# Sliding-window attention and a gated feed-forward layer on one core: q and k of six batches turned by DMA in 128-row chunks

## The chip, the cores and the metric

The kernel runs on one core of a Trainium2 chip. Its time is the device time of one launch, in microseconds (us). The engines have queues of their own and run in order: TensorE (PE in the profile; its weight loads are PEld), VectorE (DVE), ScalarE (ACT), GpSimd (POOL) and SyncE (SP, which here only issues DMAs). An instruction that waits for another engine or for a DMA holds everything behind it on its own engine.

## The reference

Eight batches of eight heads, 576 rows, 64 columns a head. Each row attends to itself and the 63 rows before it. The attention's output, as 4608 tokens of 512, goes through a layer with the gate h cos(h).

```python
scores = scale * np.matmul(q, k.transpose(0, 1, 3, 2))     # (8, 8, 576, 576)
rel = pos[:, None] - pos[None, :]
scores = np.where((rel >= 0) & (rel < 64), scores, -1e9)
attn = softmax(scores)                                     # over the last axis
x = np.matmul(attn, v)  ->  (4608, 512)
h = x @ w_in                                               # (512, 2048)
out = (h * np.cos(h)) @ w_out                              # (2048, 512), float32
```

## The kernel before

The tokens are worked in nine blocks (`mt`) of 512. In each block, the first layer runs over 16 steps `ff` (line 341: four matmuls of 128x512 into one PSUM bank, five banks in rotation by `H_BANKS`); after each step ScalarE takes the sine (line 486), and VectorE multiplies it with h from PSUM (gT, line 489), which frees the bank. The second layer follows (line 501), 64 matmuls of 128x512.

The attention of batch t+1 is woven into block t. A batch has nine query blocks `j` of 64 rows for each of four pairs of heads `p`. The scores of one (p, j) are one matmul (line 248): the stationary operand is a block of q, `qB`, 128x128 with the two heads of the pair on the diagonal and zeros beside them, so that both heads' scores come out of one matmul; the moving operand is two neighbouring 64-row blocks of k. Both must have the head's columns on the partitions, while they lie in memory with the rows there: they have to be turned. Up to four units form a group: scores, a masked maximum on VectorE (line 268), exponentials on ScalarE (line 279), the product with the inverse sum on GpSimd (line 293, result w), and turning of w, by a DMA transpose from SP (line 305) or, for the first groups, by PE (line 302). The turned weights wT and v give the next block's input on PE (line 320).

How q and k are turned:

- Batches 0 and 1: by PE from a layout of their own (line 177), untouched by the change.
- q of batches 2 to 7: loaded by GpSimd's DMAs in six chunks of 96 rows (`load_chunk`, line 146), turned by PE, six transposes for each pair (line 180), and copied from PSUM by VectorE into `qB`, one copy for each head of the pair (`put_block`, through line 113).
- k of batch 2: the same loads, PE transposes, then copies on ScalarE.
- k of batches 3 to 7: the same loads, then six DMA transposes from SP (`turn_k`, line 213).

The order of all this is set by hand. `at(time, fn, ...)` puts a step on a plan, with a time in units of which a block has T = 32: 16 for the first layer's steps and 16 for groups of four second-layer matmuls. `pump(time)` emits every planned step that is due, between matmuls. Nothing is reordered afterwards: each engine's queue follows that order. Eight DMAs of SP and eight of GpSimd may be under way at a time; the ninth waits for the first to land.

SP's queue holds turns of w, turns of k, stores of the output, and two copies of v. GpSimd's holds all loads, the products of line 293, and copies of v.

Of the kernel before, what the change touches and what calls it, by code (L numbers as in the profile page):

```python
# [15 lines left out]
BF16 = mybir.dt.bfloat16  # L16
# [5 lines left out]
NEG = -8.0e9  # L22
BIG = 3.0e38
NU = 9
NC, NP = 6, 96
GF = 4
LAST = 384
PACE = 0.36
# [9 lines left out]
RC = 9  # L38
PAIRS = 4
Q = 16  # L40
T = 2 * Q
# [17 lines left out]
def kernel(  # L59
# [35 lines left out]
    ident = const.tile([128, 128], BF16, name="ident")  # L95
# [5 lines left out]
    st = {}  # L101
# [7 lines left out]
    def bank(which, name):  # L109
        return ps.tile([128, 512], F32, tag=which, name=name)  # L110

    def copy(engine, out, in_):
        {"a": nc.scalar.copy, "p": nc.gpsimd.tensor_copy}.get(engine, nc.vector.tensor_copy)(out, in_)  # L113
# [16 lines left out]


    def rows_tile(name):
        return ld.tile([128, NC * H * D], BF16, tag=name, name=name)

    def load_heads(name, b, p0=0, n=PAIRS):
        if (name, b) not in st:
# [4 lines left out]

    def load_chunk(name, b, c):
        if (name, b) not in st:
            st[name, b] = rows_tile(name)[0:NP].rearrange("p (c x) -> p c x", c=NC)
        src = {"q": q, "k": k}[name][b, :, c * NP:c * NP + NP]
        nc.gpsimd.dma_start(out=st[name, b][:, c].rearrange("p (h d) -> p h d", h=H),  # L146
                            in_=src.rearrange("h p d -> p h d"))

    def load_v(b, c):
# [20 lines left out]
    def transposed(name, b, p):  # L170
        t_ps = ps_t.tile([128, S], BF16, tag="t", name=f"t{name}_ps")
        of = st[name, b]
        if b < 2:
            for c in range(RC):
                for h in range(2):
                    d = slice(64 * h, 64 * h + 64)
                    nc.tensor.transpose(t_ps[d, 64 * c:64 * c + 64], of[d, p, 64 * c:64 * c + 64], ident[d, d])  # L177
        else:
            for c in range(NC):
                nc.tensor.transpose(t_ps[:, NP * c:NP * c + NP], of[:, c, 128 * p:128 * p + 128], ident[:NP, :NP])  # L180
        return t_ps


    def in_order(t_ps, to, b):
        return (t_ps.rearrange("d (c p) -> d p c", c=RC), to.rearrange("d (p c) -> d p c", c=RC)) if b < 2 else (t_ps, to)

    def tr_q(b, p):
        st["tq", b, p] = transposed("q", b, p)

    def put_q(b, p, engine=None):  # L190
        of, to = in_order(st.pop(("tq", b, p)), qtiles[b * PAIRS + p], b)
        if b:
            copy(engine, to, of)
        elif engine == "a":
            nc.scalar.mul(to, of, scale)
        else:
            nc.vector.tensor_scalar(to, of, scale, None, ALU.mult)

    def put_block(b, p, h):
        d = slice(64 * h, 64 * h + 64)  # L200
        copy("d", qblocks[(b % 2) * PAIRS + p][d, :, h], st["tq", b, p][d].rearrange("d (j t) -> d j t", j=NU))

    def tr_k(b, p):
        st["tk", b, p] = transposed("k", b, p)

    def k_tile(b):
        if ("kA", b) not in st:
            st["kA", b] = ka = att.tile([128, PAIRS, S], BF16, tag="kT", name="kT", bufs=2)
            st.update({("kT", b, p): ka[:, p] for p in range(PAIRS)})
        return st["kA", b]  # L210

    def turn_k(b, c):
        nc.sync.dma_start(out=k_tile(b)[:, :, c * NP:c * NP + NP], in_=st["k", b][:, c], transpose=True)

    def put_k(b, p, engine="a"):
        kt = k_tile(b)[:, p]
        of, to = in_order(st.pop(("tk", b, p)), kt, b)
        copy(engine, to, of)


# [1 line left out]
    n_first = len(groups)  # L222
# [9 lines left out]
    def g_scores(n, which):  # L232
        s_ps = bank(S_FIRST[which] if n < n_first else S_BANKS[which], "s_ps")
        units = groups[n]
        s_ps = s_ps[:, 0:len(units) * 128].rearrange("p (u c) -> p u c", c=128)
        if n < n_first:
            m0 = 2 if units[0][2] else 0
            nc.tensor.matmul(out=s_ps.rearrange("p u c -> p (u c)"), lhsT=ident,
                             rhs=mask16[:, m0:m0 + len(units)].rearrange("p u c -> p (u c)"),
                             start=True, stop=False, skip_group_check=True)  # L240
        for u, (b, p, j) in enumerate(units):
            kt = st["kT", b, p]
            lo = max(64 * j - 64, 0)
            rhs = kt[:, lo:lo + 128].rearrange("d (a t) -> d a t", a=2)
            if j and j % 2 == 0:
                rhs = rhs[:, ::-1, :]
            if b > 1:
                nc.tensor.matmul(out=s_ps[:, u].rearrange("p (a t) -> p a t", a=2),  # L248
                                 lhsT=qblocks[(b % 2) * PAIRS + p][:, j].rearrange("d h t -> d (h t)"), rhs=rhs,
                                 start=True, stop=True, skip_group_check=True)  # L250
                continue
            for h in range(2):
                d = slice(64 * h, 64 * h + 64)
                nc.tensor.matmul(out=s_ps[d, u].rearrange("p (a t) -> p a t", a=2),  # L254
                                 lhsT=qtiles[b * PAIRS + p][d, 64 * j:64 * j + 64], rhs=rhs[d], start=n >= n_first,
                                 stop=n >= n_first or u == len(units) - 1, skip_group_check=True)
        st["s", n] = s_ps

# [73 lines left out]
    def exp_table():  # L332
        nc.scalar.activation(small, small, AF.Exp, scale=0.0)
# [12 lines left out]
            first(mt, ff, ks, n == 0, n == PAIRS - 1)  # L346

    def clear(i):
        nc.gpsimd.memset(qblocks[i].rearrange("d j h t -> d (j h t)"), 0.0)

    def last_rows(gT, o_sb):
        ms = MT // 128 - 1
# [15 lines left out]
    def at(time, fn, *args):  # L368
        plan.append((time, len(plan), fn, args))
# [9 lines left out]
    n = n_first  # L379
# [14 lines left out]

    for b in range(1, B):
        t0 = T * (b - 1)
        for p in range(PAIRS):
# [4 lines left out]
            for lag, fn, *args in steps:  # L402
                at(t_q + lag, fn, b, p, *args)
        if b > 1:
            for c in range(NC):
                for i, name in enumerate(("q", "k")):
                    at(t0 - T + (5.6 + 1.6 * c + 0.8 * i if b > 2 else 27.5 + 0.9 * c if i else 4 + 0.5 * c), load_chunk, name, b, c)
            for c in range(NC if b > 2 else 0):
                at(t0 - 5.5 + c, turn_k, b, c)
            for c in range(5):  # L410
                at(t0 + 0.5 + c, load_v, b, c)
            for half in range(2):
                at(t0 + (14.45 + 0.1 * half if b > 2 else 10), spread_v, b, half, "p" if b > 2 else "dma")
    for half in range(2):
        at(17.5, spread_v, 1, half, "dma")
    for p in range(PAIRS):
        at(T + 3 + 4 * p, clear, PAIRS + p)
# [10 lines left out]

    nc.vector.memset(small, 0.0)
    exp_table()  # L430
    for t in qblocks[:PAIRS]:
        nc.vector.memset(t.rearrange("d j h t -> d (j h t)"), 0.0)
    make_identity(nc, ident)
    load_heads("q", 0, 0, 1)
    load_heads("k", 0, 0, 1)
# [9 lines left out]
    def load():  # L445
# [21 lines left out]
    for mt in range(n_mt):  # L467
# [73 lines left out]
```

## Time and profile before

| what | value |
|---|---|
| three runs, median (lowest, highest) | 318.83 us (317.51, 319.81) |
| span of the profiled execution, first to last instruction | 316.6 us |
| granted TensorE clock, mean | 0.995 |
| PE, VectorE, ScalarE, GpSimd busy | 300.1, 227.8, 238.3, 196.6 us |
| load queue's packets (q0), and SP's (q1), share of 16 DMA engines | 75.7%, 32.5% |
| turn of a 96-row chunk of k, issue to landing, median | 6.0 us |
| turn of w, issue to landing, median | 2.9 us |

The profile is of one execution; the runs are others. No time of the profiled execution as a whole is given apart from its span, which lies 2.2 us below the median of the runs: what lies around the span, and the differences between executions, make that up. A busy engine need not be the limit, and the idle time of one that is not the limit costs nothing; the share of a DMA queue counts its packets' times, which overlap, so that shares add up to more than 100%.

### The profile page before, as it was taken

The numbers are of one execution on the slowest core, as the hardware profiler recorded it, in microseconds if no ns is written. First come the engines' busy times: TensorE is split into PE (matmuls) and PEld (weight loads), VectorE is DVE, ScalarE is ACT, GpSimd is POOL, SyncE is SP. The second block draws the span as 40 slices with busy tenths as digits, with TensorE's granted clock in tenths as the row PEclk, the third lists the DMA queues.
The fourth block names the chain that finished last, engine by engine and source line by source line (L and its number), as shares of the span: only waits on it lengthen the run. The fifth ranks groups of instructions, "written<-read, shape, count | busy, mean of one in ns | idle before, by whom it ended". The sixth has DMA issues, their size and how long they took to land.

```text
span 316.6 us, 7858 instructions
## 1 busy us (share of the span) xinstructions
PE 300.1 (95%) x2580; PEld 157.5 (50%) x2620; DVE 227.8 (72%) x871; ACT 238.3 (75%) x789; POOL 196.6 (62%) x228
## 2 busy tenths in 40 slices
PE   3678999999999999999999999999999999999995
PEld 2544545555555544545554555555555554454443
DVE  5976778689767977697859885997599758335801
ACT  3978689868998689869986998699868996115600
POOL 8896156799969767897788878986832630000000
PEclk9979999999999999999999999999999999999999
DMA  6999996699959994899989997999692442011011
GB/s 97 170 211 207 207 148 90 70 194 162 160 92 98 151 228 85 88 153 231 124 91 140 230 123 83 158 218 127 77 179 92 81 105 100 2 66 69 0 66 66
DMA packets 150697, 39.91 MB, mean 126 GB/s; under 512 B 139392, under 2 KB 146176, under 8 KB 150656
## 3 DMA queue, kind: packets, MB, share of 16 engines
q0 software_dynamic: 99824, 18.36, 75.7%
q1 hardware_dynamic: 50688, 20.85, 32.5%
q8 instruction: 20, 0.33, 0.4%
q14 instruction: 21, 0.17, 0.2%
q10 hardware_dynamic: 144, 0.20, 0.2%
HBM read 36.70 MB, written 9.44 MB: 146 GB/s over the span
## 4 chain that ended last, share of the span: by engine, by line
PE 81%; DVE 6%; ACT 5%; POOL 3%; issue 2%; DMA 2%; POOLq 0%
PE h_ps L341 35%; PE out_ps L501 34%; ACT e L279 3%; PE s_ps L248 3%; DVE gT L489 3%; PE o_ps L320 3%; DMA k<-in_k_dram 2%; PE tq_ps L180 2%; PE s_ps L254 1%; POOL w L293 1%; PE out_ps L356 1%; DVE qB L113 1%; PE tw_ps L302 1%; POOL v L113 1%; PE tk_ps L177 1%
## 5 line engine op out<-in xcount | busy, mean ns | idle before, releaser
L341 PE MATMUL h_ps<-xT,w_in 128*128 128x512 bf16 x556 | 130.5, 379 | 2.9 <-ACT xT L113 1.0
L501 PE MATMUL out_ps<-w_out,gT 128*128 128x512 bf16 x543 | 130.9, 379 | 1.2 <-issue 0.5
L486 ACT ACTIVATE sin<-h_ps 128x512 f32<-128x512 f32 x144 | 83.6, 598 | 39.2 <-PE h_ps L341 36.2
L489 DVE TENSOR_TENSOR gT<-h_ps,sin 128x512 bf16<-128x512 f32 x144 | 92.2, 685 | 27.1 <-ACT sin L486 26.2
L279 ACT ACTIVATE e<-s,negm 128x128 f32<-128x128 f32 x256 | 98.7, 388 | 1.0 <-DVE negm L268 0.9
L293 POOL TENSOR_TENSOR w<-e,rden 128x512 bf16<-128x512 f32 (+1 forms) x78 | 74.0, 958 | 35.6 <-DVE rden L286 29.1
L341 PEld LDWEIGHTS <-w_in 128*128 128x128 bf16 x576 | 54.3, 98 | 60.7 <-issue 2.4
L501 PEld LDWEIGHTS <-gT 128*128 128x128 bf16 x560 | 51.5, 98 | 49.7
L268 DVE CUSTOM_DVE_ANT_0 s<-s_ps,mask 128x128 f32<-128x128 f32 x256 | 58.2, 285 | 1.9 <-PE s_ps L254 1.6
L279 ACT ACTIVATION_READ_ACCUMULATOR e<-s,negm 128x1 f32 x256 | 48.1, 188 | 0.0
L146 POOL DMA_DIRECT2D q<-in_q_dram x36 | 28.9, 804 | 12.3 <-PE h_ps L341 4.7
L152 POOL DMA_DIRECT2D v<-in_v_dram x40 | 34.1, 874 | 3.0 <-DMA k<-in_k_dram 2.0
L146 POOL DMA_DIRECT2D k<-in_k_dram x36 | 29.0, 806 | 3.2 <-DMA k<-in_k_dram 2.4
L113 ACT COPY out_sb<-out_ps 128x512 f32<-128x512 f32 (+1 forms) x18 | 10.1, 563 | 25.7 <-PE out_ps L501 20.2
L286 DVE RECIPROCAL rden<-den 128x4 f32<-128x4 f32 (+1 forms) x80 | 13.9, 173 | 20.9 <-ACT e L279 18.3
L113 DVE CAST xT<-o_ps 128x512 bf16<-128x512 f32 x27 | 17.5, 678 | 9.9 <-PE o_ps L320 9.9
L113 DVE COPY out_sb<-out_ps 128x512 f32<-128x512 f32 x18 | 12.4, 689 | 16.6 <-PE out_ps L501 12.6
L248 PEld LDWEIGHTS <-qB 128*128 128x128 bf16 x216 | 17.0, 98 | 14.6 <-DVE negm L268 0.6
L113 POOL COPY v<-v 64x2048 bf16<-64x2048 bf16 (+1 forms) x11 | 18.7, 1701 | 5.4 <-DMA v<-in_v_dram 5.0
L248 PE MATMUL s_ps<-kT,qB 128*128 128x128 bf16 x216 | 21.9, 219 | 0.2 <-DVE negm L268 0.2
L113 DVE COPY qB<-tq_ps 64x576 bf16<-64x576 bf16 x48 | 21.6, 450 | 0.3
L268 DVE DVE_READ_ACCUMULATOR2_ANT negm<- 128x1 f32 x256 | 21.3, 83 | 0.0
(57 smaller groups left out, 187.5 us busy)
## 6 DMA issues: line engine op xcount, KB each, us to landing
out_dram<-out_sb SPq DMA_DIRECT2D x16, 512.0 KB, 6.8
v<-in_v_dram POOLq DMA_DIRECT2D x32, 128.0 KB, 6.2
q<-in_q_dram POOLq DMA_DIRECT2D x36, 96.0 KB, 7.1
k<-in_k_dram POOLq DMA_DIRECT2D x36, 96.0 KB, 7.5
w_out<-in_moe_w_out_dram POOLq DMA_DIRECT2D x2, 1024.0 KB, 16.4
w_in<-in_moe_w_in_dram POOLq DMA_DIRECT2D x2, 768.0 KB, 11.8
wT<-w SPq DMA_TRANSPOSE x66, 2.9
out_dram<-out_sb SPq DMA_DIRECT2D x3, 256.0 KB, 2.0
```

Source lines behind the costliest of these rows:

```text
L113: {"a": nc.scalar.copy, "p": nc.gpsimd.tensor_copy}.get(engine, nc.vector.tensor_copy)(out, in_)
L146: nc.gpsimd.dma_start(out=st[name, b][:, c].rearrange("p (h d) -> p h d", h=H), in_=src.rearrange("h p d -> p h d"))
L152: nc.gpsimd.dma_start(out=vt.rearrange("p (h d) -> p h d", h=H), in_=v[b, :, c * 128:c * 128 + n, :].rearrange("h p d -> p h d"))
L248: nc.tensor.matmul(out=s_ps[:, u].rearrange("p (a t) -> p a t", a=2), lhsT=qblocks[(b % 2) * PAIRS + p][:, j].rearrange("d h t -> d (h t)" ...
L268: nc.vector.tensor_tensor_reduce(out=s[:, u], in0=s_ps[:, u], in1=mask[:, 2 - j % 2 if j else 0], scale=-scale if b else -1.0, scalar=BIG, ...
L279: nc.scalar.activation(e[:, u], s[:, u], AF.Exp, bias=negm[:, u:u + 1], scale=1.0 if n < n_first else -1.0, accum_out=den[:, u:u + 1])
L286: nc.vector.reciprocal(out=rden[:, 0:len(groups[n])], in_=den[:, 0:len(groups[n])])
L293: (nc.gpsimd if engine == "p" else nc.vector).tensor_tensor(out=w[:, 0:u], in0=e[:, 0:u], op=ALU.mult, in1=rden[:, 0:u].unsqueeze(2).to_br ...
L341: nc.tensor.matmul(out=st["h", ff], lhsT=w_in_sb[:, ks, ff * 128:ff * 128 + 128], rhs=st["xT", mt][:, ks], start=start, stop=stop)
L486: nc.scalar.activation(sin, h_ps, AF.Sin, bias=math.pi / 2.0)
L489: nc.vector.tensor_tensor(out=gt[:, e], in0=h_ps, in1=sin, op=ALU.mult)
L501: nc.tensor.matmul(out=o_ps[e], lhsT=gT[ff // 2][:, ff % 2, ms * 128:ms * 128 + 128], rhs=w_out_sb[:, ff], start=ff == 0, stop=ff == n_ff - 1)
```

## The change

q and k of batches 2 to 7 are handled alike. Each is loaded in five chunks (four of 128 rows, one of 64) and turned by three DMA transposes from SP: chunks 0 and 1, chunks 2 and 3, chunk 4 (`turn`). The turned tile has the order chunk, pair, row. VectorE then copies turned q, from SBUF, to its blocks, four copies for a batch: for each head of the pairs, chunks 0 to 3 together and chunk 4 alone (`spread_q`). `qB` is one tile for each parity of the batch in place of four, with its blocks in another order; `q_block` and `k_blocks` find the operands of a score matmul in the new orders. Batches 0 and 1 keep their way; their turned q lies in the rotating tiles of tag X.

In the plan of a batch b (t0 = 32 (b - 1)), the k turns stand at t0 - 5.5, -4.9 and -4.3, the q turns at -3.7, -3.1 and -2.5, and the copies to the blocks at t0 + 6.2, 7.2, 8.2 and 9.2. The loads of batch 2 stand together at 4 to 8.5 of the first block, k first; before, its k was loaded at 27.5 to 32.

```diff
-NC, NP = 6, 96
+NC = 5
...
-    qtiles = [const.tile([128, S], BF16, name=f"qT{i}") for i in range(2 * PAIRS)]
-    qblocks = [const.tile([128, NU, 2, 64], BF16, name=f"qB{i}") for i in range(2 * PAIRS)]
+    qblocks = [const.tile([128, NU * PAIRS, 2, 64], BF16, name=f"qB{i}") for i in range(2)]
...
-        src = {"q": q, "k": k}[name][b, :, c * NP:c * NP + NP]
+        n = min(128, S - 128 * c)
+        src = {"q": q, "k": k}[name][b, :, c * 128:c * 128 + n]
...
-    def put_block(b, p, h):
-        d = slice(64 * h, 64 * h + 64)
-        copy("d", qblocks[(b % 2) * PAIRS + p][d, :, h], st["tq", b, p][d].rearrange("d (j t) -> d j t", j=NU))
...
-    def turn_k(b, c):
-        nc.sync.dma_start(out=k_tile(b)[:, :, c * NP:c * NP + NP], in_=st["k", b][:, c], transpose=True)
+    def turn(name, b, lo, hi):
+        key = name + "X", b
+        if key not in st:
+            st[key] = att.tile([128, NC, PAIRS, 128], BF16, tag="X" if name == "q" else "kT", name=name + "X", bufs=2)
+        n = min(128, S - 128 * lo)
+        nc.sync.dma_start(out=st[key][:, lo:hi, :, 0:n].rearrange("d c a t -> d (c a) t"),
+                          in_=st[name, b][:n, lo:hi].rearrange("p c x -> p (c x)"), transpose=True)
+
+    def spread_q(b, h, lo, hi):
+        d = slice(64 * h, 64 * h + 64)
+        of, n = st["qX", b], 2 if hi < NC else 1
+        to = qblocks[b % 2][d, 2 * PAIRS * lo:2 * PAIRS * lo + n * PAIRS * (hi - lo), h]
+        nc.vector.tensor_copy(to.rearrange("d (m i) t -> d m i t", i=n),
+                              of[d, lo:hi, :, 0:64 * n].rearrange("d c a (i t) -> d (c a) i t", i=n))
...
-            if b > 1:
-                nc.tensor.matmul(out=s_ps[:, u].rearrange("p (a t) -> p a t", a=2),
-                                 lhsT=qblocks[(b % 2) * PAIRS + p][:, j].rearrange("d h t -> d (h t)"), rhs=rhs,
-                                 start=True, stop=True, skip_group_check=True)
+            if b > 1:
+                nc.tensor.matmul(out=s_ps[:, u].rearrange("p (a t) -> p a t", a=2), lhsT=q_block(b, p, j),
+                                 rhs=k_blocks(b, p, j), start=True, stop=True, skip_group_check=True)
...
-            t_q = 7 + 1.8 * p if b == 1 else t0 + 1 + 2.5 * p if b == 2 else t0 + 1 + 3.5 * p
-            steps = (((0, tr_q), (0.01, tr_k), (0.02, put_q), (0.03, put_k)) if b == 1 else
-                     ((0, tr_q), (0.02, put_block, 0), (0.5, put_block, 1)) +
-                     (((9.5 - 0.8 * p, tr_k), (9.51 - 0.8 * p, put_k)) if b == 2 else ()))
...
-                    at(t0 - T + (5.6 + 1.6 * c + 0.8 * i if b > 2 else 27.5 + 0.9 * c if i else 4 + 0.5 * c), load_chunk, name, b, c)
-            for c in range(NC if b > 2 else 0):
-                at(t0 - 5.5 + c, turn_k, b, c)
+            for i, name in enumerate(("k", "q")):
+                for c in range(NC):
+                    at((4 + 0.5 * c + 2.5 * i if b == 2 else t0 - T + 5.6 + 1.8 * c + 0.9 * i), load_chunk, name, b, c)
+                for c, (lo, hi) in enumerate(((0, 2), (2, 4), (4, 5))):
+                    at(t0 - 5.5 + 1.8 * i + 0.6 * c, turn, name, b, lo, hi)
+            for c, (lo, hi) in enumerate(((0, 4), (4, 5))):
+                for h in range(2):
+                    at(t0 + 6.2 + h + 2 * c, spread_q, b, h, lo, hi)
```

More of the change, by code (lines that the diff above doesn't have):

```diff
@@ L143, in load_chunk @@
         if (name, b) not in st:
-            st[name, b] = rows_tile(name)[0:NP].rearrange("p (c x) -> p c x", c=NC)
-        src = {"q": q, "k": k}[name][b, :, c * NP:c * NP + NP]
-        nc.gpsimd.dma_start(out=st[name, b][:, c].rearrange("p (h d) -> p h d", h=H),
+            st[name, b] = rows_tile(name).rearrange("p (c x) -> p c x", c=NC)
+        n = min(128, S - 128 * c)
+        src = {"q": q, "k": k}[name][b, :, c * 128:c * 128 + n]
+        nc.gpsimd.dma_start(out=st[name, b][:n, c].rearrange("p (h d) -> p h d", h=H),
                             in_=src.rearrange("h p d -> p h d"))
@@ L172, in transposed, with in_order, q_tile @@
         of = st[name, b]
-        if b < 2:
-            for c in range(RC):
-                for h in range(2):
-                    d = slice(64 * h, 64 * h + 64)
[L177 to L180, printed above, removed]
-        return t_ps
-    def in_order(t_ps, to, b):
-        return (t_ps.rearrange("d (c p) -> d p c", c=RC), to.rearrange("d (p c) -> d p c", c=RC)) if b < 2 else (t_ps, to)
+        for c in range(RC):
+            for h in range(2):
+                d = slice(64 * h, 64 * h + 64)
+                nc.tensor.transpose(t_ps[d, 64 * c:64 * c + 64], of[d, p, 64 * c:64 * c + 64], ident[d, d])
+        return t_ps
+    def in_order(t_ps, to):
+        return t_ps.rearrange("d (c p) -> d p c", c=RC), to.rearrange("d (p c) -> d p c", c=RC)
+    def q_tile(b):
+        if ("qT", b) not in st:
+            st["qT", b] = att.tile([128, PAIRS, S], BF16, tag="X", name="qT", bufs=2)
+        return st["qT", b]
     def tr_q(b, p):
@@ L206, in k_tile, with q_block, k_blocks @@
     def k_tile(b):
[L207 to L210, printed above, removed]
-    def turn_k(b, c):
-        nc.sync.dma_start(out=k_tile(b)[:, :, c * NP:c * NP + NP], in_=st["k", b][:, c], transpose=True)
+        if ("kT", b) not in st:
+            st["kT", b] = att.tile([128, PAIRS, S], BF16, tag="kT", name="kT", bufs=2)
+        return st["kT", b]
+    def turn(name, b, lo, hi):
[6 more added lines that the diff above has]
+    def spread_q(b, h, lo, hi):
+        d = slice(64 * h, 64 * h + 64)
+        of, n = st["qX", b], 2 if hi < NC else 1
+        to = qblocks[b % 2][d, 2 * PAIRS * lo:2 * PAIRS * lo + n * PAIRS * (hi - lo), h]
+        nc.vector.tensor_copy(to.rearrange("d (m i) t -> d m i t", i=n),
+                              of[d, lo:hi, :, 0:64 * n].rearrange("d c a (i t) -> d (c a) i t", i=n))
+    def q_block(b, p, j):
+        u = PAIRS * (j - j % 2) + (2 * p + j % 2 if j + 1 < NU else p)
+        return qblocks[b % 2][:, u].rearrange("d h t -> d (h t)")
+    def k_blocks(b, p, j):
+        blocks = st["kX", b].rearrange("d c a (i t) -> d (c a i) t", i=2)
+        if j % 2 or j == 0:
+            u = 4 * (j - j % 2) + 2 * p
+            return blocks[:, u:u + 2]
+        u = 4 * j + 2 * p
+        return blocks[:, u - 7:u + 1:7][:, ::-1]
     def put_k(b, p, engine="a"):
-        kt = k_tile(b)[:, p]
-        of, to = in_order(st.pop(("tk", b, p)), kt, b)
+        of, to = in_order(st.pop(("tk", b, p)), k_tile(b)[:, p])
         copy(engine, to, of)
@@ L254, in g_scores @@
                 nc.tensor.matmul(out=s_ps[d, u].rearrange("p (a t) -> p a t", a=2),
-                                 lhsT=qtiles[b * PAIRS + p][d, 64 * j:64 * j + 64], rhs=rhs[d], start=n >= n_first,
+                                 lhsT=q_tile(b)[d, p, 64 * j:64 * j + 64], rhs=rhs[d], start=n >= n_first,
                                  stop=n >= n_first or u == len(units) - 1, skip_group_check=True)
@@ L396 @@
         t0 = T * (b - 1)
-        for p in range(PAIRS):
-            t_q = 7 + 1.8 * p if b == 1 else t0 + 1 + 2.5 * p if b == 2 else t0 + 1 + 3.5 * p
-            steps = (((0, tr_q), (0.01, tr_k), (0.02, put_q), (0.03, put_k)) if b == 1 else
-                     ((0, tr_q), (0.02, put_block, 0), (0.5, put_block, 1)) +
-                     (((9.5 - 0.8 * p, tr_k), (9.51 - 0.8 * p, put_k)) if b == 2 else ()))
[L402 to L406, printed above, removed]
-                    at(t0 - T + (5.6 + 1.6 * c + 0.8 * i if b > 2 else 27.5 + 0.9 * c if i else 4 + 0.5 * c), load_chunk, name, b, c)
-            for c in range(NC if b > 2 else 0):
-                at(t0 - 5.5 + c, turn_k, b, c)
+        if b == 1:
+            for p in range(PAIRS):
+                for lag, fn in ((0, tr_q), (0.01, tr_k), (0.02, put_q), (0.03, put_k)):
+                    at(7 + 1.8 * p + lag, fn, b, p)
+        else:
+            for i, name in enumerate(("k", "q")):
[4 more added lines that the diff above has]
+            for c, (lo, hi) in enumerate(((0, 4), (4, 5))):
+                for h in range(2):
+                    at(t0 + 6.2 + h + 2 * c, spread_q, b, h, lo, hi)
             for c in range(5):
@@ L416 @@
     for p in range(PAIRS):
[L417 removed]
+        at(T + 3 + 4 * p, clear, p)
     for mt in range(1, n_mt):
@@ L430 @@
     exp_table()
-    for t in qblocks[:PAIRS]:
-        nc.vector.memset(t.rearrange("d j h t -> d (j h t)"), 0.0)
+    for p in range(PAIRS):
+        nc.vector.memset(qblocks[0][:, NU * p:NU * p + NU].rearrange("d j h t -> d (j h t)"), 0.0)
     make_identity(nc, ident)
```

12 lines of the change are left out of this document (5 added, 7 removed).

## The prediction

> **What bounds the kernel now.** Times of the trace are us from the start of the span. I read the busy shares first, then the chain that ended last. The shares put TensorE (PE) far ahead, and the chain is mostly the two large matmul lines, L341 (first layer) and L501 (second layer).
>
> ```profile
> PE 300.1 (95%) x2580; PEld 157.5 (50%) x2620; DVE 227.8 (72%) x871; ACT 238.3 (75%) x789; POOL 196.6 (62%) x228
> PE 81%; DVE 6%; ACT 5%; POOL 3%; issue 2%; DMA 2%; POOLq 0%
> ```
>
> Then the same by block of 512 tokens (windows; columns: length, busy of PE, PE weight loads, VectorE, ScalarE, GpSimd, clock, DMA share, GB/s):
>
> ```profile
> 95.00:129.00 34.00, 33.42 (x287) 17.38 (x286) 26.08 (x114) 28.59 (x98) 26.40 (x31) 1.00 1.31 138
> 160.60:192.60 32.00, 31.78 (x248) 16.61 (x252) 25.50 (x113) 27.52 (x96) 26.23 (x29) 1.00 1.51 147
> ```
>
> A block takes 32.0 us with PE busy in all of it: PE time removed there is time gained, a PE stall is time lost. The DMA share above 1 says that packets of several queues overlap and queue for the whole block.
>
> **PE: what is removed.** PE's timeline gives the price of the turning: six transposes of one pair stand between two runs of first-layer matmuls.
>
> ```profile
> 163.22 0.42 PE L180 MATMUL tq_ps<-ident,q 96*128 96x96 bf16 x6
> 163.47 2.76 PE L341 MATMUL h_ps<-xT,w_in 128*128 128x512 bf16 x12
> ```
>
> The next run starts 0.255 us after the first transpose, so one costs 42.5 ns on PE. Gone are 144 for q (batches 2 to 7) and 24 for k of batch 2: 168 x 42.5 ns = **-7.1 us**. The score matmuls keep count and shape (216 at 128x128), so I price their new operands at nothing. The four ScalarE copies of k for batch 2 go too; ScalarE has room.
>
> **VectorE.** 48 copies from PSUM of 0.45 us (21.6) go. In come 24 `spread_q`: per batch two of 64x2048 and two of 64x256. No such copy is in the trace. The nearest row, SBUF to SBUF in bf16 on 64 partitions:
>
> ```profile
> L113 DVE COPY v<-v x1: 1233/1233/1233, 19.1 to 19.1; 64x1536 bf16<-64x1536 bf16 x1
> ```
>
> That is 0.80 ns an element: **c = 1.64 us** for 64x2048, 0.2 for 64x256. The low end is 0.2 us, a copy of 64 columns (mask, 195 ns); that one ran beside a GpSimd instruction, so 1.64 is also the high end. I take 1.64, being the only row of this kind. In sum 12 x 1.64 + 12 x 0.2 = 22: VectorE is not relieved. Here the Trainium skill says otherwise: "VectorE: DVE Perf Modes", section "The perf-mode tier table", gives 693 ns for 2048 bf16 elements in SBUF, four a cycle; by it the final sum would be 9.5 us lower. The 1233 ns for 1536 contradicts it, on one sample.
>
> **The wait that is added.** PE's q transposes read SBUF loaded a block earlier and waited for nothing. Now q passes SyncE's queue (SP), and VectorE's in-order stream waits for it: the first `spread_q` stands behind gT of step 7 in each block and needs the second q turn. Where is that turn? In the order of the changed kernel, SP's sequence from the first k turn on is k, k, k, w, q, w, **q**, q, w in blocks 4 to 6 (w is a turn of softmax weights); in blocks 2 and 3 one w stands earlier. In all five blocks 2 to 6 the second q turn is the seventh transpose, counted from the first turn of k. Before, SP also had nine there (six of k, three of w), so I read its timeline at the same place (block 5, first L341 matmul at P = 192.62):
>
> ```profile
> 190.98 3.19 SPq L213 DMA_TRANSPOSE kT<-k  x2
> 194.28 1.20 SPq L305 DMA_TRANSPOSE wT<-w  x1
> 195.56 1.21 SPq L213 DMA_TRANSPOSE kT<-k  x1
> 196.88 1.24 SPq L305 DMA_TRANSPOSE wT<-w  x1
> 198.21 2.54 SPq L213 DMA_TRANSPOSE kT<-k  x2
> ```
>
> One transpose costs SP 1.2 us, back to back, whether 96 or 128 rows, 384 or 512 columns; I take 1.2 for 1024 columns too (2.4 at most). The seventh starts at 199.5. And it lands late, for instance in block 4 (P = 160.59):
>
> ```profile
> L213 SPq DMA_TRANSPOSE kT<-k x1: 1207/1207/1207, 168.3 to 168.3; - x1
> ...
> DMA to landing us min/median/max: 7.2/7.2/7.2
> ```
>
> The seventh starts at 102.5, 136.9, 168.3, 199.5, 231.5 and lands 7.1, 7.0, 7.2, 6.8, 4.4 us later. With P = 95.6, 129.25, 160.6, 192.6, 224.6 that is L = P + 14.0, 14.65, 14.9, 13.7 and 11.3, summing to 68.5. (v and the next batch's q and k load from P+1 on; block 6 has only v to load.) For k this was harmless: scores start at P+14.9 and need the late chunks later still. For `spread_q` it is not: gT of step 7 ends near P+8.
>
> **From the wait to PE.** While VectorE waits, PE runs on until it has no bank: the first layer rotates over five, and step 13 needs the bank of step 8, step 15 that of step 11. VectorE after L: large copy, gT 8, large copy, gT 9, small, gT 10, small, gT 11. With gT at 0.62 apart (2.48 for four) PE may start step 15 at L + 2c + 2.9; undisturbed it starts at P + 15 x 4 x 0.216 = P + 13.0. Stall of a block: (L-P) + 2c - 10.1, which with c = 1.64 gives 7.2, 7.9, 8.1, 6.9, 4.5, together **+34.5 us**. It returns in every block: SP's row of turns hangs on the scores of the block before, not on the stalled half, and PE has no slack to win it back. Block 1 (batch 2) is spared: no load runs between 52 and 65 us, and its q turns, issued near 63 to 66, land before 70.
>
> **GpSimd.** Batch 2's k loads move from between the softmax products (58.9 to 66) to ahead of them. GpSimd's queue was already the limit there, and PE took its product w 0.2 us after it was ready:
>
> ```profile
> 42.80 3.82 POOL L146 DMA_DIRECT2D q<-in_q_dram  x5 [4.52 <-DMA w_out<-in_moe_w_out_dram]
> 46.63 1.05 POOL L293 TENSOR_TENSOR w<-e,rden 128x512 bf16<-128x512 f32 x1
> ```
>
> PE's transpose of w starts at 47.88. With nine loads after 42.8 instead of five, at 0.87 for 128 rows (the v row) and 0.7 for the 64-row one, the queue frees at 50.3; w ends at 51.35; PE waits **+3.5 us**, once. Other batches issue ten loads for twelve (about 1 us less of GpSimd).
>
> Block 2 took 33.7 us (95.59 to 129.25) against 32.0, the 5.0 us in which GpSimd waited for v being part of it; behind a stall of 7 us that excess is covered: **-1.6**.
>
> **Sum.** 316.6 - 7.1 + 34.5 + 3.5 - 1.6 = 345.9 us of span. The median of the runs, 318.83, lies 2.2 above this span (0.9 to 3.2 for the three), so **348 us**.
>
> **Ends.** c from 0.2 to 1.64 moves the sum by 14.4 at most (348 down to 334). L has both sides open: below.
>
> **Rivals.**
> (a) Bytes, not turns, set the landing. A two-chunk turn moves 256 KB against 96. If each of the turns in the crowded stretch (about two and a half up to the second q) counts as two at 1.9 us, the mean gap between landings there (164.7 to 178.1, seven of them), L moves 4.7 later: 5 x 4.7 = +23.5, near 371. For it: the DMA engines are full. Against: turns of w with 384 and 512 columns landed at like gaps.
> (b) A partial stall. Fewer, larger DMAs, or a cheap copy, bring L to P+10 or 11: 1 to 3 us a block, 320 to 333.
> (c) No stall: the decisive point is L + 2c = P + 10.1. A k turn outside the crowd landed in 2.4 us (the shortest); issued by P+5 and landing so, q is there in time and only -7.1 + 3.5 remain, 315.2; without GpSimd's wait, 311.7. The Trainium skill would have it so: "Advanced Engine Details and Errata", section "X-Bar Transpose (TRN2)", says transposing DMAs are as fast as regular ones, 350 to 400 GB/s; an estimate from that page is 0.75 us for 256 KB. The rows against (c): 30 turns of 96 KB with a median of 6.0 us to landing.
> That the turns do not replace PE's work is ruled out by the order of the changed kernel.
>
> **Chances.** Forecast with its ends (333 to 357) 0.50; (a) 0.20; (b) 0.17; (c) 0.13. The range leaves out (c) and the far end of (a): 320 to 372. A measurement here tells about 1% (3.2 us) from no change: faster 0.11, same 0.07, slower 0.82.
>
> **What would show it.** In the profile after: `spread_q`'s wait for qX as VectorE's largest new wait, some 6 us in each of five blocks; PE idle before L341 with VectorE's gT as releaser; blocks of 36 to 39 us in place of 32; L180 gone; PE waiting some 3 us for w near 48. I am wrong if qX lands by P+8, or if VectorE's waits leave PE no gap.

## The result, and the profile after

The changed kernel takes 364.52 us (median of four runs, 363.77 to 369.14) against 318.57 us for the kernel before (317.51 to 319.81): a ratio of 1.1474, 95% interval [1.1402, 1.1546]. It is slower, as forecast, and by more than the 348 us forecast. The ratios in this text are of each kernel's fast runs against the fast runs of the kernel before that were taken with them (a run over 1.5% above the fastest of its kernel counts as slow), so they can differ a little from the quotient of two medians. The profiled execution has a span of 362.4 us, 45.8 longer than before.

The page of the changed kernel, in the order in which the prediction read that of before: busy shares, granted clock by 40 slices, the chain by engine.

```profile
PE 304.8 (84%) x2413; PEld 152.9 (42%) x2452; DVE 227.7 (63%) x847; ACT 235.9 (65%) x785; POOL 194.0 (54%) x216
...
PEclk9999978999998699958999699988999899999999
...
PE 32%; DMA 27%; POOL 18%; issue 15%; DVE 5%; ACT 2%; SPq 0%; POOLq 0%; DVEq 0%
```

VectorE's work has hardly moved (227.7 against 227.8 us). PE has 167 instructions fewer and yet is busy 4.7 us longer, and the clock row shows why: it dips again and again, where before it dipped only at the start. PE's share of the chain falls from 81% to 32%; DMA (27%), GpSimd (18%) and time that the profile puts down to no releaser ("issue", 15%) took its place.

The largest new waits, from the answer on who waited for whom (us in total, times, longest):

```profile
PEld L359 <- issue: 52.6, 50, 9.1
POOL w L311 <- issue: 44.7, 5, 10.1
ACT sin L504 <- DVE gT L507: 42.7, 10, 9.1
DVE qB L221 <- DMA qX<-q: 40.3, 6, 9.4
...
PE h_ps L359 <- DVE gT L507: 37.6, 11, 8.8
```

The first row is the weight loads of matmuls that cannot start yet. The rows that matter are six waits of VectorE for turned q, 40.3 us, and behind them eleven of PE for gT, 37.6 us. One of them, in block 3 (P = 141.87, the first L359 matmul), on the timeline of VectorE and then of PE:

```profile
159.69 1.72 DVE L221 COPY qB<-qX 64x2048 bf16<-64x2048 bf16 x1 [9.39 <-DMA qX<-q]
161.33 0.67 DVE L507 TENSOR_TENSOR gT<-h_ps,sin 128x512 bf16<-128x512 f32 x1
162.04 1.67 DVE L221 COPY qB<-qX 64x2048 bf16<-64x2048 bf16 x1
163.74 0.69 DVE L507 TENSOR_TENSOR gT<-h_ps,sin 128x512 bf16<-128x512 f32 x1
```
```profile
162.06 1.01 PE L359 MATMUL h_ps<-xT,w_in 128*128 128x512 bf16 x2 [8.81 <-DVE gT L507]
163.29 0.63 PE L359 MATMUL h_ps<-xT,w_in 128*128 128x512 bf16 x1 [0.22 <-issue]
164.49 2.08 PE L359 MATMUL h_ps<-xT,w_in 128*128 128x512 bf16 x5 [0.56 <-DVE gT L507]
```

VectorE stands 9.39 us, copies, makes gT of step 8 (161.33), and PE goes on with step 13 after a pause of 8.81 us. After the pause its matmuls take 2.08 / 5 = 0.42 us each instead of 0.216 at the full clock. SP's row for block 5 (P = 225.06), at the place where the prediction read that of before:

```profile
223.43 5.06 SPq L213 DMA_TRANSPOSE kX<-k  x3
228.59 1.20 SPq L323 DMA_TRANSPOSE wT<-w  x1
229.89 1.38 SPq L213 DMA_TRANSPOSE qX<-q  x1
231.38 1.60 SPq L323 DMA_TRANSPOSE wT<-w  x1
233.08 3.39 SPq L213 DMA_TRANSPOSE qX<-q  x2
```

The second q turn is the seventh transpose, as the order had it, and starts at P + 8.0. The one of block 3, by itself (2.9 us of SP, 10.5 us to landing):

```profile
L213 SPq DMA_TRANSPOSE qX<-q x1: 2884/2884/2884, 149.2 to 149.2; - x1
...
DMA to landing us min/median/max: 10.5/10.5/10.5
```

Last, the blocks by windows (length, busy of PE, PE weight loads, VectorE, ScalarE, GpSimd, clock, DMA share, GB/s):

```profile
67.80:100.70 32.90, 31.77 (x258) 16.05 (x260) 24.74 (x111) 27.38 (x95) 27.19 (x29) 1.00 1.49 168
100.70:141.90 41.20, 33.67 (x227) 16.33 (x230) 25.90 (x109) 27.59 (x96) 25.59 (x27) 0.88 1.19 124
141.90:184.20 42.30, 32.52 (x225) 15.93 (x229) 26.36 (x109) 27.01 (x95) 25.80 (x27) 0.88 1.17 123
```

Block lengths, from the first first-layer matmul of each block to that of the next:

| block | 0 | 1 | 2 | 3 | 4 | 5 | 6 | 7 | 8 |
|---|---|---|---|---|---|---|---|---|---|
| before, us | 39.64 | 33.77 | 32.45 | 32.55 | 32.03 | 31.99 | 31.99 | 28.86 | 31.12 |
| after, us | 45.82 | 32.98 | 41.13 | 42.33 | 40.86 | 40.84 | 36.89 | 28.86 | 30.74 |

Of the 45.8 us, blocks 2 to 6 hold 41.0 and block 0 holds 6.2; block 1, the last block and the start give 1.4 back.

### The profile page after: what moved, and what is told of

The parts are those of the page before. It is cut to its first block, busy times and chain, and to the rows that moved or that the text cites. A ratio compares the mean times of both kernels' runs of the same rounds, so it can differ in the third digit from the quotient of the medians.

```text
span 362.4 us, 7495 instructions
## 1 busy us (share of the span) xinstructions
PE 304.8 (84%) x2413; PEld 152.9 (42%) x2452; DVE 227.7 (63%) x847; ACT 235.9 (65%) x785; POOL 194.0 (54%) x216
## 4 chain that ended last, share of the span: by engine, by line
PE 32%; DMA 27%; POOL 18%; issue 15%; DVE 5%; ACT 2%; SPq 0%; POOLq 0%; DVEq 0%
PE out_ps L519 17%; DMA qX<-q 14%; POOL w L311 10%; PE h_ps L359 10%; DMA v<-in_v_dram 5%; DMA w_out<-in_moe_w_out_dram 5%; POOL v L112 2%; DVE qB L221 2%; ACT e L297 2%; DMA q<-in_q_dram 2%; DVE gT L507 2%; PE o_ps L338 1%; POOL v L152 1%; PE s_ps L263 1%; DMA kX<-k 1%
## 5 line engine op out<-in xcount | busy, mean ns | idle before, releaser
L359 PE MATMUL h_ps<-xT,w_in 128*128 128x512 bf16 x557 | 136.0, 396 | 40.3 <-DVE gT L507 37.6
L507 DVE TENSOR_TENSOR gT<-h_ps,sin 128x512 bf16<-128x512 f32 x144 | 93.6, 686 | 29.5 <-ACT sin L504 29.1
L359 PEld LDWEIGHTS <-w_in 128*128 128x128 bf16 x576 | 57.4, 101 | 112.0 <-issue 52.6
L221 DVE COPY qB<-qX 64x2048 bf16<-64x2048 bf16 (+1 forms) x24 | 18.0, 751 | 40.6 <-DMA qX<-q 40.3
L146 POOL DMA_DIRECT2D k<-in_k_dram x30 | 26.8, 894 | 13.8 <-PE h_ps L359 5.0
L146 POOL DMA_DIRECT2D q<-in_q_dram x30 | 26.8, 900 | 4.6 <-DMA q<-in_q_dram 4.3
L112 ACT COPY out_sb<-out_ps 128x512 f32<-128x512 f32 (+1 forms) x18 | 10.2, 566 | 27.0 <-PE out_ps L519 21.5
L304 DVE RECIPROCAL rden<-den 128x4 f32<-128x4 f32 (+1 forms) x80 | 13.9, 173 | 20.7 <-ACT e L297 19.1
L112 DVE CAST xT<-o_ps 128x512 bf16<-128x512 f32 x27 | 17.5, 679 | 11.3 <-PE o_ps L338 11.3
L112 POOL COPY v<-v 64x2048 bf16<-64x2048 bf16 (+1 forms) x11 | 20.1, 1832 | 5.4 <-DMA v<-in_v_dram 5.1
L263 PE MATMUL s_ps<-kX,qB 128*128 128x128 bf16 x216 | 22.0, 220 | 0.0
## 6 DMA issues: line engine op xcount, KB each, us to landing
q<-in_q_dram POOLq DMA_DIRECT2D x24, 128.0 KB, 10.2
w_out<-in_moe_w_out_dram POOLq DMA_DIRECT2D x2, 1024.0 KB, 16.5
w_in<-in_moe_w_in_dram POOLq DMA_DIRECT2D x2, 768.0 KB, 11.8
```

Of the source, the lines that this page charges most:

```text
L146: nc.gpsimd.dma_start(out=st[name, b][:n, c].rearrange("p (h d) -> p h d", h=H), in_=src.rearrange("h p d -> p h d"))
L221: nc.vector.tensor_copy(to.rearrange("d (m i) t -> d m i t", i=n), of[d, lo:hi, :, 0:64 * n].rearrange("d c a (i t) -> d (c a) i t", i=n))
L359: nc.tensor.matmul(out=st["h", ff], lhsT=w_in_sb[:, ks, ff * 128:ff * 128 + 128], rhs=st["xT", mt][:, ks], start=start, stop=stop)
L507: nc.vector.tensor_tensor(out=gt[:, e], in0=h_ps, in1=sin, op=ALU.mult)
```

## The experiments

The theory is the prediction's: VectorE's in-order wait for the second q turn stops gT, and gT stops PE. Still to be told apart were: the wait or the copies and the fuller DMA engines; what sets the late landing (place in SP's row, number of turns, bytes, the loads beside them); and block 0. Every edit is made on the changed kernel unless another is named. L is the landing of the second q turn, counted from P.

### e1: q's turns ahead of k's

```diff
-at(t0 - 5.5 + 1.8 * i + 0.6 * c, turn, name, b, lo, hi)
+at(t0 - 5.5 + 1.8 * (1 - i) + 0.6 * c, turn, name, b, lo, hi)
```

> Edit: in each batch the three q turns stand ahead of the three k turns on SP; all else as changed. Theory A (the time is VectorE's wait for the second q turn, which is the seventh in SP's row): the second q turn becomes the second or third, is issued before the block's loads fill the DMA engines and lands before P+8, so that VectorE does not wait; five blocks lose their stalls (41.1, 42.3, 40.9, 40.8, 36.9 us go to 31 to 33), and the span falls from 362.4 to 318 to 326. Theory B (the turns as such are too much for the DMA engines, whichever comes first): k then lands as late as q did, near P+17, where scores want its later chunks, and PE stalls there instead: 335 or more.

Measured: 329.18 us (median, 327.74 to 330.52), ratio to before 1.0345 [1.0298, 1.0392], span 328.3. L falls to P+3.6 to 8.1, VectorE's wait for qX is gone, blocks 2 to 6 take 34.6, 33.9, 33.8, 32.6, 33.5 us. The place in SP's row alone is worth 34 of the 46 us. The blocks are up to 1.6 us over the 31 to 33 expected and the span 2.3 us over its range. A wait that was not on the list goes with this:

```profile
DVE out_sb L112 <- DMA out_dram<-out_sb: 14.3, 4, 4.2
```

The stores of a block stand on SP behind its turns. With blocks of 41 us they had landed in time (the changed kernel has no such wait); with blocks of 33 us VectorE waits for them before it can empty the second layer's banks into the same two buffers, and the softmax behind it is late: PE waits 6.3 us for negm, the masked maximum.

### e10: the same turns and copies, without the wait

```diff
-        of, n = st["qX", b], 2 if hi < NC else 1
+        of, n = st["qX", b] if b == 2 else st["kX", b - 1], 2 if hi < NC else 1
```

> From batch 3 on, spread_q copies rows of the k of the batch before (already turned a block ago) into q's blocks; the q of batches 3 to 7 is still loaded and turned, but not used. So every load, every turn and every copy stays, and only VectorE's wait for this block's q turn is gone (block 1 keeps its own). Theory (the wait is the loss): blocks 2 to 6 fall from 41.1, 42.3, 40.9, 40.8, 36.9 us to 32 to 33.5, PE's clock stays full in blocks 3 to 6, span 318 to 326. Rival (the copies themselves, or the fuller DMA engines, hold PE back): the blocks stay above 36, span over 340.

Measured: 335.56 us (one run), span 333.8. Blocks 2 to 6: 34.2, 34.3, 33.4, 35.4, 32.5 us, 169.9 in all against 202.1, although the q turns still land at P+12 to P+19. Windows of blocks 3 and 4:

```profile
138.60:172.80 34.20, 31.22 (x231) 15.46 (x229) 24.31 (x106) 26.10 (x91) 24.69 (x27) 1.00 1.54 152
172.80:206.30 33.50, 31.41 (x231) 15.59 (x230) 24.38 (x107) 27.45 (x96) 25.95 (x27) 1.00 1.47 158
```

The full clock is back in these two blocks, and PE's busy time falls to 31.2 to 31.4 us. So the wait, not the copies nor the DMA engines, makes the blocks long. The span missed its range. The trace shows three things that lengthen it: the wait for stores appears here too (15.4 us, with 8.3 us of PE waits for negm); block 5 had half the clock for 3.4 us, against the full clock expected; and block 1, which still waits for its own q, took 38.7 us instead of 33.0. Up to there this kernel does what the changed one does; its q landed at P+11.6 instead of P+10.4. Block 1 sits on the edge.

### e8 and e6: fewer and more turns for the same bytes

```diff
-for c, (lo, hi) in enumerate(((0, 2), (2, 4), (4, 5))):    # the turns
+for c, (lo, hi) in enumerate(((0, 4), (4, 5))):            # e8
+for c, (lo, hi) in enumerate(((0, 1), (1, 2), (2, 3), (3, 4), (4, 5))):    # e6, 0.36 apart instead of 0.6
```

> Chunks 0 to 3 are turned by one transpose of 512 KB instead of two of 256 KB, so a batch has four turns in place of six with the same bytes, and the q that spread_q needs is the fourth or fifth of SP's row instead of the seventh. Theory of the prediction (the number of turns sets the landing, about 1.9 us each): it lands some 3.8 us earlier, near P+12 to P+13.5, blocks 2 to 5 near 37 to 38 us, span 342 to 348. Rival (a) of the prediction (bytes set the landing): it lands at P+16 to P+17.5 as before, blocks 40 to 42, span 357 to 364.

> One chunk per transpose: ten turns of 128 KB (64 KB the last) in place of six for each batch, the same bytes. Theory of the prediction (the number of turns sets the landing): the fourth q turn, which spread_q now waits for, stands four places later in SP's row and lands about 7 us later, P+22 to P+25; blocks 2 to 5 near 47 to 49 us, span 385 to 398. Rival (a) (bytes set the landing): it lands at P+16 to P+18, span 360 to 367.

Measured: e8 358.53 us (span 356.8), e6 378.64 us (span 376.9), one run each. Neither theory holds by itself: L is 16.0, 15.6, 15.4, 13.2 in e8 (15.7, 17.8, 17.2, 17.0 with six turns) and 21.2, 20.7, 19.4, 19.8 in e6. Taken apart into issue and time to landing, blocks 2 to 5, for the last turn that the large copies need:

| turn | kernel | issued, P + | issue to landing, us | mean |
|---|---|---|---|---|
| 96 KB (k) | before, seventh | 6.9, 8.8, 7.7, 6.9 | 7.1, 7.0, 7.2, 6.8 | 7.0 |
| 128 KB | e6 | 13.4, 13.1, 11.9, 12.1 | 7.8, 7.5, 7.5, 7.7 | 7.7 |
| 256 KB | changed | 6.4, 7.3, 8.1, 8.0 | 9.3, 10.5, 9.1, 8.9 | 9.5 |
| 512 KB | e8 | 5.0, 3.9, 3.9, 3.9 | 11.0, 11.6, 11.5, 9.3 | 10.8 |

The number of turns sets when SP issues the one that counts; its size sets how long it is under way, and less than in proportion (from 96 to 512 KB, 7.0 to 10.8 us). Fewer turns gain at the first and lose at the second.

### e2: no loads of q and k from batch 4 on

```diff
+        if b > 3:
+            st[name, b] = st[name, b - 2]        # turn the rows of batch 2 or 3 again
...
-                for c in range(NC):
+                for c in range(NC if b < 4 else 0):
```

> Edit: q and k of batches 4 to 7 are not loaded; batches 4 and 6 turn the rows of batch 2 again, 5 and 7 those of batch 3 (part of the input is left out). The turns, their order and v's loads stay. In blocks 2 to 5 the DMA engines then have v alone to load beside the turns. If the loads make the turns late, the second q turn lands near P+11 to 13 in blocks 2 to 5, as it does in block 6 (P+13.0), these blocks take 36 to 37 us, and the span is near 344. If SP's own row of transposes sets it (issue one by one, 256 KB each), it lands at P+16 to 18 as now, and the span stays at 362.

Measured: 351.12 us (one run), span 349.3. L in blocks 2 to 6 is P+11.0, 13.8, 13.4, 12.6, 13.3; the second q turn takes 5.5, 7.4, 5.9, 5.8, 5.7 us to land instead of the 9.5 above. The loads beside it are 3 to 4 us of its lateness. The landings came as expected; the span is 5 us longer than expected because block 1, with its q at P+10.5 and large copies of 1.2 and 1.5 us, took 38.4 us: the edge seen in e10 too.

### e3 and e4: batch 2's k loads back between the softmax products

```diff
-at((4 + 0.5 * c + 2.5 * i if b == 2 else ...), load_chunk, name, b, c)
+at((4 + 0.5 * c if i else 27.5 + 0.9 * c) if b == 2 else ..., load_chunk, name, b, c)
...
-at(t0 - 5.5 + 1.8 * i + 0.6 * c, turn, name, b, lo, hi)
+at(t0 + 1.5 + 0.6 * c if b == 2 and not i else t0 - 5.5 + 1.8 * i + 0.6 * c, turn, name, b, lo, hi)
```

e4 is this together with e1's order of the turns.

> Edit: the five k loads of batch 2 go back to where they stood before (27.5 to 31.1 of the plan), its q loads to 4 to 6, and its k turns to the start of block 1. Theory: the 3.8 us in which PE waits for w near 48 us go, and with them the half clock that PE was granted for 6.8 us from 49.9 on, which took some 2.2 us more: span 356 to 357. If the half clock has another cause, only the 3.8 us go: 358.6. If GpSimd's queue is not what PE waits for: 362.

> Both edits: q turns first, and batch 2's k loads and turns late. Theory A: what is left of the change is PE's 7.1 us without the waits: 310 to 316 of span, 312 to 318 of time, that is 0 to 2% below the kernel before. Theory B: 330 or more.

Measured: e3 356.88 us (one run), span 355.1; block 0 falls from 45.82 to 39.35 us. The wait that goes is this one, on PE's timeline of the changed kernel:

```profile
51.31 0.61 PE L320 MATMUL tw_ps<-ident,w 128*128 128x128 bf16 x4 [3.78 <-POOL w L311]
```

It is 3.8 of the 6.5 us. The other 2.7 go with a stretch at half clock, which the changed kernel has there and e3 has not: of its 6.8 us, 5.4 lie behind the pause, and half of 5.4 is 2.7. e4: 324.02 us (322.41 to 325.62), ratio 1.0201 [1.0155, 1.0246], span 320.6, above the 310 to 316 expected. The two parts add up: e3 has 7.3 us less span than the changed kernel, e4 7.7 less than e1. Still about 2% slower than before; left over are 9.5 us of waits for stores (with 4.0 us of PE waits for negm), 2.8 us of PE in block 1 for turned weights, and 0.4 us of PE in each of blocks 3 to 6 at P+1.2, where it waits for ScalarE's copy of xT. The expectation of e14 puts these 0.4 us at the first large copy of q; the trace of e4 has no gap of PE there.

### e14: e4 with a third output buffer

```diff
-            o_sb = moe.tile([128, 2, d_model], F32, tag="out", name="out_sb", bufs=2)
+            o_sb = moe.tile([128, 2, d_model], F32, tag="out", name="out_sb", bufs=3)
```

> The kernel of e4 with a third output buffer and nothing else, to part the steps of e11. Theory (the stores that land late behind the turns hold VectorE's output copy, and through it the softmax): VectorE's 9.5 us of waiting for stores and the 4.0 us of PE waits for negm behind it go, the 0.4 us PE gap at the first large copy to q's blocks stays in each block, block 1 stays near 36 us; span 316 to 318. Rival (the halved copies or batch 2's earlier turns made most of e11's 7 us): span 319 to 321.

Measured: ratio 0.9966 [0.9934, 0.9998], span 316.7. The waits for stores are gone, and 3.9 us of span with them; blocks 2, 3 and 5 take 31.2 us, and the 0.4 us gaps, which were expected to stay, are gone too. In block 4 the second q turn landed at P+9.8, VectorE waited 1.5 us, and the block took 33.7.

The change frees the eight qT tiles, 9.2 KB of a partition, of which the third buffer takes 4.1. On the kernel before a third buffer was not tried. Its own trace has such waits too:

```profile
DVE out_sb L113 <- DMA out_dram<-out_sb: 3.9, 3, 2.3
```

But PE waited only 0.2 us for negm there, so by an estimate from these two waits it would gain little.

### e9, e11, e12: what is left

e9 is e14 with the large copies in halves of 64x1024 and batch 2's last q turn later; e11 is e9 with all of batch 2's q turns ahead of block 0's turns of weights; e12 is e11 with the q turns of the later batches one place earlier in SP's row.

```diff
-            for c, (lo, hi) in enumerate(((0, 4), (4, 5))):            # the copies
+            for c, (lo, hi) in enumerate(((0, 2), (2, 4), (4, 5))):
                 for h in range(2):
-                    at(t0 + 6.2 + h + 2 * c, spread_q, b, h, lo, hi)
+                    at(t0 + 5.2 + h + 2 * c, spread_q, b, h, lo, hi)
```

The times of the turns in e14, e9, e11 and e12, one line each:

```diff
-at(t0 + 1.5 + 0.6 * c if b == 2 and not i else t0 - 5.5 + 1.8 * (1 - i) + 0.6 * c, turn, ...)
+at(t0 + 1.5 + 0.6 * c if b == 2 and not i else t0 + 1.2 if b == 2 and c == 2 else t0 - 5.5 + 1.8 * (1 - i) + 0.6 * c, turn, ...)
+at((t0 + 1.5 if not i else t0 - 10) + 0.6 * c if b == 2 else t0 - 5.5 + 1.8 * (1 - i) + 0.6 * c, turn, ...)
+at((t0 + 1.5 if not i else t0 - 10) + 0.6 * c if b == 2 else (t0 - 6.5 if i else t0 - 3.7) + 0.6 * c, turn, ...)
```

> The kernel of e4 (q's turns first, batch 2's k loads late) with three changes against its leftover waits: three output buffers instead of two, batch 2's last q turn behind the weights of its block, and the large copies to q's blocks in halves (64x1024 each, one between two gT). Theory: VectorE's wait for the stores (9.5 us in e4, with 4 us of PE behind it) falls below 2 us, block 1 loses about 1 us, the steady blocks come to 31 to 32 us; span 314 to 318, a ratio to the kernel before of 0.99 to 1.01. Rival (late stores were only the last of several late things): PE waits elsewhere for the same 4 to 6 us, span 319 to 322.

> The kernel of e9 with batch 2's three q turns moved ahead of all turns of weights of block 0 (they are issued near 48 to 53 us, where no load runs) instead of among them. In e9 a w turn behind the first q turn took 6.6 us and PE waited 2.8 us for it, and block 1 took 37.8 us. Theory: block 1 falls to 32 to 34 us, the steady blocks stay at 31 to 32, span 311 to 315, ratio to the kernel before 0.98 to 0.995. Rival (batch 2's turns only move the queue in front of batch 1's weights): block 0 or block 1 grows by the same 3 to 5 us, span 317 to 321.

> The kernel of e11 with the q turns of batches 3 to 7 one turn of weights earlier in SP's row. In e9 the second q turn of block 4 landed at P+11.8 and VectorE waited 1.9 us for it, with 3.6 us of PE behind it; in the other blocks at P+5 to P+6. Theory: no q turn lands after P+7, no block after the second is over 32.5 us, span 310 to 314. Rival (the turns of weights that slip behind are needed first): PE waits for wT instead, 1 to 3 us in some blocks, span 314 to 318.

Measured: the four runs of e9 took 315.07, 320.85, 321.37 and 322.63 us, too far apart for a ratio; the profiled one, 320.85, has a span of 319.1, above the 314 to 318 expected. In it blocks 2, 3 and 5 take 31.0 us without a gap, but in block 4 the second q turn came at P+11.8, and block 1 took 37.8 (35.3 in e14). In block 1 PE waited 2.8 us for turned weights, as in e14, but here the clock was at half for 3.4 us around the end of that wait, and PE waited 1.0 us more behind VectorE's gT. Why the four runs differ was not shown, and nothing here speaks for the later place of that turn.

e11 goes the other way: ratio to before **0.9865 [0.9835, 0.9896]**, median 314.70 us (six runs, 312.68 to 317.90), span 313.6; block 1 takes 34.9, blocks 2 to 6 take 31.0, 31.3, 31.9, 31.0, 32.3.

e12: ratio 0.9893 [0.9866, 0.9921], median 315.04 us (six runs, 313.56 to 321.15), span 313.7; its second q turns all land by P+5.7 and no later block is over 32.5 us, as expected, though third turns still landed at P+7.1 to P+10.4 in three blocks; for the weights that slipped behind PE waited 0.9 us in block 1 and 0.2 in block 5, less than the rival's 1 to 3. The two kernels' intervals overlap, so the earlier place is worth nothing that these runs can tell. Blocks 3 and 5 of e11 by windows:

```profile
127.50:158.80 31.30, 30.89 (x226) 15.65 (x228) 25.02 (x111) 27.62 (x96) 25.58 (x28) 1.00 1.71 162
190.70:221.70 31.00, 30.77 (x224) 15.60 (x228) 24.72 (x111) 26.97 (x95) 25.81 (x27) 1.00 1.63 170
```

31.00 against 31.99 us before: this is the PE time that the change was able to give, and e11 gets it in blocks 2 and 5, and most of it in 3. How much of the 3.1 us of span between e14 and e11 belongs to the halved copies and how much to the earlier turns was not parted.

## Why the prediction was right, and where its sizes were off

The direction and the mechanism came as forecast; the size only in part. 364.5 us lies outside the forecast's own ends (333 to 357) and inside the whole range because that was drawn out towards rival (a), whose 371 is nearer than 348. That the miss is not larger is luck in part: c, priced 2.9 us too high, makes up for some of what L and the clock were priced too low.

**What bounds the kernel, and the chain to PE: right.** PE has no slack, VectorE's first `spread_q` waits behind gT of step 7 for the second q turn, the turn is the seventh of SP's row, and PE stops at step 13. e1 and e10 take the wait away in two ways and lose 34 and 32 us of blocks. The formula (L-P) + 2c - 10.1 holds: with the measured L and c it gives stalls of 8.7, 11.1, 9.6, 9.3 and 5.0 us; on a block of 31.0 that is 198.7 us for blocks 2 to 6, and 202.1 were measured. In e6 it gives 207.3 (c = 0.69) against 212.0. The rests of 3.4 and 4.7 us are taken up below, with the clock.

**PE's -7.1: right.** 24 x 42.5 ns are 1.02 us a block; undisturbed blocks went from 31.99 to 31.00.

**L: mis-sized, +12.2 us.** The five landings came to 80.7 us after P, not 68.5. 1.2 of it is a misreading: block 3 of the kernel before begins at 128.04, not 129.25, where a second run of matmuls starts on the timeline. The rest is the step "lands 7.1, 7.0, 7.2, 6.8, 4.4 us later": it carried the time of a 96 KB turn over to one of 256 KB, which took 9.3, 10.5, 9.1, 8.9, 5.0. SP's issue came out as forecast (37.8 us after P in sum, 37.2 before). Rival (a) was right that bytes count, but priced them at 4.7 us a block, where 9.5 against 7.0 is 2.5.

**Block 2's -1.6: mis-sized, +0.7 us, by the same misreading.** That block took 32.45 us before, not 33.7. Blocks 2 to 6 took 161.0 before; less 5.1 us of transposes that is 155.9, against 5 x 31.0 undisturbed, so 0.9 of the 1.6 came.

**c: mis-sized, -2.9 us.** 1.64 us was forecast for each 64x2048 copy; the twelve took 1.24 in the mean, and not at one price:

```profile
L221 DVE COPY qB<-qX x24: 207/688/1737, 78.2 to 283.2; 64x2048 bf16<-64x2048 bf16 x12, 64x256 bf16<-64x256 bf16 x12
```
```profile
L221 DVE COPY qB<-qX x24: 207/656/717, 82.2 to 298.1; 64x2048 bf16<-64x2048 bf16 x12, 64x256 bf16<-64x256 bf16 x12
```

The first is the changed kernel, the second e6, where the turns land so late that GpSimd's copies of v are over: no copy is above 0.72 us. In the changed kernel seven copies had GpSimd's v copies beside them for 0.8 to 1.7 us and took 1.4 to 1.7; the four with none took 0.68 to 0.69; the last, with 0.75 us of one beside it, took 0.81. The v<-v row that the forecast rested on had run beside a product of GpSimd (18.75 to 20.97 on its timeline), so it was most likely the price of a copy beside GpSimd, and 0.69 is that of one alone. The Trainium skill's figure ("VectorE: DVE Perf Modes", section "The perf-mode tier table", 693 ns) agrees with the copies that ran alone; the prediction set it aside on one sample, of which it said itself that GpSimd ran beside it.

**GpSimd's k loads of batch 2: right, 3.8 us for 3.5.** The loads ran until 50.2 and the product w followed.

**Block 1 spared: wrong as reasoned, small in effect.** Its second q turn landed at P+10.4, not before P+8.2, with v's loads issued from P+1.5 on and the next batch's from P+6.7. With copies of 0.69 us that left 1.0 us of PE (the block took 32.98, against 33.77 less the 2.04 of its 48 transposes); with P+11.6 and slower copies (e10) it was 4.1 us, and the block 5.7 us longer.

**The clock: not in the sum.** No term was there for what a pause does to PE afterwards. It cost about 2.4 us in block 0 (45.82 less 39.64 before and the wait of 3.78) and at most 3.4 in blocks 2 to 6, the rest of the formula above; that the whole rest is the clock's was not shown.

The terms together: 12.2 (L) - 2.9 (c) + 3.4 (the rest of the formula) + 0.7 (block 2) + 2.7 (block 0: 0.3 wait, 2.4 clock) + 1.2 (block 1) - 0.6 (start and last block) = 16.7, for the 16.5 us between the forecast span of 345.9 and the 362.4 measured.

**Rivals.** (b) and (c) are out for the kernel as it is. (c)'s condition, L + 2c by P+10.1, is what decides, as e14 shows: in its block 4 the second q turn landed at P+9.8 and the copies took 0.69 us each, so L + 2c was P+11.2, 1.1 us too late, and PE waited 0.42 and 0.68 us for gT; in blocks 3 and 5, with landings at P+5.4 and P+4.2, it did not wait for it. (c)'s price without the GpSimd wait, 311.7 us, was not quite reached: e11, with q first, took 314.70. The page that (c) leaned on ("Advanced Engine Details and Errata", section "X-Bar Transpose (TRN2)", of the Trainium skill) gives a rate, 350 to 400 GB/s, which does not give the time of a single turn: by the earlier estimate 256 KB would take 0.75 us, and the quickest one here, in e4, took 3.1.

```profile
L213 SPq DMA_TRANSPOSE qX<-q x1: 1231/1231/1231, 57.2 to 57.2; - x1
...
DMA to landing us min/median/max: 3.1/3.1/3.1
```

## What to carry to other kernels

When data moves from an engine that had it in hand to a queue, find the instruction that will wait for it, count what stands ahead of it in that queue, and price the landing from transfers of its own size in the same stretch; then ask who stands behind the waiting instruction on its in-order engine. Here the saving of 1 us a block was real and became a loss of 9 because k, needed some 7 us later, was turned before q. Removing the first wait brought out the next one (stores behind the turns, two buffers). With three things put right together (q first, batch 2's k loads late, a third buffer) the kernel was level with the one before (0.9966); with the earlier turns and halved copies of e11 as well it gained 1.35%.

## What the runs showed of the hardware that was not expected

- **A pause of PE can cost more than its length.** Around its pauses of 3.8 to 8.8 us the granted clock of the changed kernel was at half for 3.4 to 10.2 us, in six places; 128x512 matmuls took 0.42 us instead of 0.216. A pause of 3.8 us cost 6.2 to 6.5 in block 0; in blocks 2 to 6 at most 3.4 us came on top of the 43.7 of the formula, since PE waits through much of the stretch at half clock. The clock row of the kernel before:

```profile
PEclk9979999999999999999999999999999999999999
```

  Against it stands the changed kernel's row at the head of this text. e10, with PE gaps of at most 2.8 us in blocks 3 and 4, has a mean of 1.00 there; e6, with 11.3 and 10.7 us in blocks 2 and 3, has 0.88. The length of the pause alone does not decide it: a pause of 2.8 us came with half the clock for 3.4 us in e9 and with none in e14, and one of 2.0 us in block 5 of e10 with 3.4 us. The Trainium skill ("TensorE: Matmul & The Clock Gate", Part 1) says that the clock is either half or full and goes by windows of 3413 ns; the stretches at half clock here are one, two or three of these.
- **The price of VectorE's SBUF copies depends on GpSimd**: in the changed kernel 0.68 to 0.69 us for 64x2048 with no GpSimd copy beside it, 0.81 to 1.74 with one. In e10 two such copies beside GpSimd's issuing of loads, one of them beside a memset too, took 1.89 and 2.25. GpSimd's own 64x2048 copies of v went from 1.89 to 2.13 us in the mean.
- **A DMA transpose under load**: 7.0, 7.7, 9.5 and 10.8 us to landing for 96, 128, 256 and 512 KB beside the loads; 6.1 for 256 KB with only v's loads beside it, 3.1 at the quickest. SP's own time for one was 1.2 us at the shortest for 96 to 256 KB, and 2.9 for the turn of block 3 shown above.
